# Left-over queries scored on 64 rows in the AV banks, and some loads issued later, in an attention + maxout FFN kernel

## The chip, the cores and the metric

One core of a Trainium2 chip runs the whole program. The metric is the device time of one execution in microseconds (us), and smaller is better. A kernel is run several times, and its median and range are given. The profile is of one of these runs. Where two kernels are compared by a ratio, it is the mean time of one kernel's fast runs over the mean time of the other's fast runs of the same rounds on the same chip, so it isn't quite the ratio of the medians that stand beside it. All runs in this document were in the fast state but one of the six of e5 (327.61 us), which its ratio leaves out and its median does not. All kernels gave a correct result.

Engines in the profile: PE is TensorE, PEld its weight loads, ACT is ScalarE, DVE is VectorE, POOL is GpSimd (it issues most of the loads), SP is SyncE (it issues transposes by DMA and stores).

## The reference, cut to what matters

Eight batches, eight heads, 576 positions, head size 64; then a three-way maxout FFN on the 4608 tokens.

```python
scores = scale * np.matmul(q, k.transpose(0, 1, 3, 2)) + bias      # bias depends on |i - j| only
attn = np.exp(scores - max); attn = attn / sum(attn)
x = (attn @ v).transpose(0, 2, 1, 3).reshape(4608, 512)
h = np.maximum(np.maximum(x @ w1, x @ w2), x @ w3)                 # d_ff = 768
out = h @ w_out
```

576 is four tiles of 128 and 64 left over. So each pair of heads has full tiles of keys and queries, left-over keys and left-over queries. The bias is applied as a multiplication after the exponential ("band products" on VectorE). The FFN of one batch runs on PE between the attention products of the next.

## The kernel before: the parts that matter

A head pair has two visits (query halves c = 0 and 1). Each makes scores in two `sc` tiles, exponentials on ScalarE, band products on VectorE, and then a "filling": FFN work put on PE while the other engines deal with the scores. Three PSUM pools of two buffers each matter: one for scores (`sc`, also used by `sct`, left-over keys, and `scq`, left-over queries), one for attention outputs (`a`, the "AV banks") and one for the FFN (`ff`).

```python
ps_s = ctx.enter_context(tc.tile_pool(name="ps_s", bufs=2, space=bass.MemoryType.PSUM))   # sc, sct, scq
ps_a = ctx.enter_context(tc.tile_pool(name="ps_a", bufs=2, space=bass.MemoryType.PSUM))   # a
ps_f = ctx.enter_context(tc.tile_pool(name="ps_f", bufs=2, space=bass.MemoryType.PSUM))   # ps0, ps1, ps2, pso
...
# one portion of filling: third product of the last block, first and second of this one
portions.append([g[fb - 1], f[fb], m[fb]])      # g: ps2 -> hT (DVE max); f: ps0 -> m0 (ACT copy); m: ps1 -> m (DVE max)
...
def left_queries(hp, qT, kT, el):
    sc = ps_s.tile([P, KT, 2 * 64], F32, tag="sc", name="scq")
    for t in range(KT):                       # both heads at once, half of the 128 rows times zeros
        mm(sc[:, t, :], lhsT=kT[:, P * t : P * t + P], rhs=qT[:, QM : QM + P])
    eq = el[:, S + 64 :].rearrange("p (t h q) -> p t h q", t=KT, h=2)
    exp(eq, sc[:].rearrange("p t (h q) -> p t h q", h=2))
...
for b, hp in ...:                             # main loop, cut
    visit(qT, kT, e4, 0)
    quotients = next_late()                   # AV products of the pair before, first half
    times_band(hp, e4, 0, 0, QS, inorder)
    quotients()
    fill(rate, lambda: left_keys(hp, qT, kT, el, 0, S + 64))
    visit(qT, kT, e4, 1)
    quotients = next_late()                   # AV products, second half
    times_band(hp, e4, 1, 0, QM, inorder)     # the band product that stands ahead of hT on VectorE
    quotients()
    ...
    def queries():
        left_queries(hp, qT, kT, el)
        times_band(hp, e4, 3, 0, QM, inorder)
    fill(rate, lambda: times_band(hp, e4, 2, 0, QM, inorder), queries)
```

Everything on PE and VectorE is pinned to this order (`inorder`).

The softmax here doesn't subtract the row's maximum and nothing guards it: scores larger than these inputs give would overflow.

Of the kernel before, what the change touches and what calls it, by code (L numbers as in the profile page):

```python
# [39 lines left out]
def kernel(  # L40
# [77 lines left out]
    def constants(i):  # L118
        inorder(nc.vector.memset(ktail[i][:], 0.0))
        if i == 0:  # L120
            inorder(nc.vector.memset(qtail[i][:], 0.0))
        inorder(nc.vector.memset(vt[i][:], 0.0))
        inorder(nc.vector.memset(vx[i][:, :, :, D:AW], 1.0))
        for par in range(2):
            inorder(nc.vector.memset(vt[i][64 * par : 64 * par + 64, :, par, D:AW], 1.0))
# [7 lines left out]
    def in_turn(b, load):  # L133
        return inorder(load) if b > 2 else load

    def load_main(src, b, h0, h1, dst, t0=0, t1=KT):
        x = main_part(src, b)
        if h1 - h0 < KT:
            for h in range(h0, h1):
                nc.gpsimd.dma_start(out=dst[:, :, h, :], in_=x[:, :, h, :])  # L140
        else:
            for t in range(t0, t1):
                in_turn(b, nc.gpsimd.dma_start(out=dst[:, t, h0:h1, :], in_=x[:, t, h0:h1, :]))  # L143
# [5 lines left out]
    def q_diag(b, par, h0, h1):  # L149
        return diag(qtail[b % 2], par, h0, h1)  # L150
# [7 lines left out]
    def load_tail(src, b, h0, h1, dst):  # L158
        for par in range(2):
            in_turn(b, nc.gpsimd.dma_start(out=dst(b, par, h0, h1), in_=tail_part(src, b, h0, h1, par)))  # L160

    def load_qk(b, behind=None):
# [5 lines left out]
        for src, dst in ((q, q_diag), (k, k_diag)):  # L168
            for par in range(2):
                load = nc.gpsimd.dma_start(out=dst(b, par, 0, H), in_=tail_part(src, b, 0, H, par))  # L170
                loads.append(in_turn(b, load))
        if behind:
            for load in loads:
                tc.add_manual_dep(
                    load.ins, behind.ins.name,
                    mybir.DependencyInfo(mybir.DependencyClass.Sync, mybir.DependencyReason.DATA),
                    reason="these loads go behind the result's transposes",
                )

    def load_v(b, h0, h1):  # L180
        load_main(v, b, h0, h1, vx[b % 2][:, :, :, 0:D])
        load_tail(v, b, h0, h1, v_diag)
# [61 lines left out]
    inorder(nc.vector.memset(qtail[1][:], 0.0))  # L244
# [17 lines left out]
    load_tail(q, 0, 0, H, q_diag)  # L262
# [40 lines left out]
    bandt = const.tile([P, HP, 2 * P], BF16, name="bandt")  # L303

    def make_bandt():
        for par in range(2):
            r = slice(64 * par, 64 * par + 64)
            c = BAND // 2 - 64 * par
            for c0, c1 in ((192, 256), (0, 192)):
                dve_copy(bandt[r, :, c0:c1], hank[r, par::2, c : c + c1 - c0][:, :, ::-1])  # L310
# [4 lines left out]
    def ffn(t0, nt, last):  # L315
# [76 lines left out]
        else:  # L392
# [3 lines left out]
            portions.append(o[:1])  # L396
# [4 lines left out]
    pending, rest, stores = [], [], []  # L401
# [36 lines left out]
    def transposes(b):  # L438
# [4 lines left out]
        def one(j, t):  # L443
            src = batch[b][j][:, t].rearrange("p h d -> p (h d)") if t < KT else (
                (qtail, ktail)[j][b % 2][:].rearrange("p h c -> p (h c)")
            )
            inorder(nc.sync.dma_start_transpose(out=made[j][:, :, P * t : P * t + P], in_=src))
# [6 lines left out]
    def qk_tiles():  # L454
        return [qkt.tile([P, HP, (KT + 1) * P], BF16, tag=n, name=n) for n in ("qT", "kT")]
# [25 lines left out]
    def more_transposes(hp):  # L481
# [6 lines left out]
        dve_copy(qk[0][0][:, hp, QS:], tp[:, 0 : QS + P])  # L488

    def second_transposes(made, hp):  # L490
# [3 lines left out]
        for j, tl in enumerate((qtail, ktail)):  # L494
# [11 lines left out]
            copy(made[j][:, hp, KT * P :], tp[:, j, KT * P : (KT + 1) * P])  # L506
            for j, copy in enumerate((dve_copy, act_copy))
# [16 lines left out]
    def visit(qT, kT, e4, c, mid=None):  # L524


        for tt in range(0, KT, 2):
# [23 lines left out]
    def times_bandt(hp, el):  # L551
        inorder(nc.vector.tensor_tensor(
            out=el[:, S - 192 : S + 64], in0=el[:, S - 192 : S + 64], in1=bandt[:, hp, :], op=ALU.mult
        ))

    def left_queries(hp, qT, kT, el):

        sc = ps_s.tile([P, KT, 2 * 64], F32, tag="sc", name="scq")
        for t in range(KT):
# [314 lines left out]
```

## Time and profile before

| kernel before | |
|---|---|
| time, median of 4 runs (3 of them known when the prediction was made) | 325.96 us (323.77 to 326.36) |
| span of the profiled run | 324.3 us |
| PE busy | 310.4 us, 96% of the span |
| one batch in the steady part (start of batch five to start of batch six) | 33.88 us |
| longest wait of PE | 3.43 us, at 16.3 to 19.7 us, on the values' tail `vt` |
| half-speed stretches of PE's clock | two of 3.41 us, from 19.59 and 29.83 us (granted clock 0.50 in both) |

Busy shares tell that PE is the engine whose stream is the time, and the start of the same instruction in two successive batches gives the length of a batch without any adding up. Most lines of the page and the timelines are in the prediction below. One row that it doesn't show, of the costliest groups (after the bars: busy us, mean ns of one, idle us before them and what ended it):

```profile
L94 PE MATMUL ps<-xT,w_bf 128*128 128x512 bf16 (+1 forms) x720 | 156.4, 359 | 0.0
```

Half of PE's busy time is these FFN products, and PE never waited in front of one. In a timeline the columns are start, duration, engine, source line, operation, written tile <- read tiles, shapes, count, and in brackets the idle time before with what ended it.

### The profile page before, as it was taken

How to read it: one execution, taken by the hardware profiler on the slowest of the kernel's cores; microseconds unless marked ns; L12 is line 12 of the kernel's file. 1: busy time of each engine (PE TensorE's matmuls, PEld its weight loads, DVE VectorE, ACT ScalarE, POOL GpSimd, SP SyncE). 2: the span in 40 equal slices, each digit the busy share in tenths (PEclk: the TensorE clock that was granted, in tenths of full speed). 3: DMA queues.
4: the chain of work that ended last, by engine and by line, in shares of the span. 5: the costliest groups of instructions: out<-in, count | busy, mean ns of one | idle time of the engine just before them, and what ended most of it. 6: DMA issues, size and time to landing. Idle time of an engine off the chain costs nothing.

```text
span 324.3 us, 8019 instructions
## 1 busy us (share of the span) xinstructions
PE 310.4 (96%) x3232; PEld 177.1 (55%) x3232; DVE 216.0 (67%) x537; ACT 201.8 (62%) x274; POOL 112.6 (35%) x151
## 2 busy tenths in 40 slices
PE   7757999999999999999999999999999999999995
PEld 2345776787555555555555555555555554444442
DVE  6476787777666766676667766777767675454452
ACT  3947798798677667776777677667776651121221
POOL 8941977109857852194109700500000000000000
PEclk9978999999999999999999999999999999999999
DMA  9999999949999999999989998996032003301103
GB/s 163 188 207 198 154 162 153 164 109 127 192 160 155 159 181 168 118 129 164 200 81 127 175 209 76 104 205 119 1 73 98 35 3 73 132 0 65 67 0 129
DMA packets 165541, 40.72 MB, mean 126 GB/s; under 512 B 155384, under 2 KB 161024, under 8 KB 165504
## 3 DMA queue, kind: packets, MB, share of 16 engines
q0 software_dynamic: 103904, 16.66, 74.8%
q1 hardware_dynamic: 59840, 23.08, 38.7%
q10 hardware_dynamic: 1760, 0.47, 0.6%
q8 instruction: 25, 0.41, 0.5%
q14 instruction: 12, 0.10, 0.1%
HBM read 35.39 MB, written 9.45 MB: 138 GB/s over the span
## 4 chain that ended last, share of the span: by engine, by line
PE 86%; ACT 4%; POOL 3%; DMA 3%; DVE 2%; issue 1%; POOLq 0%; ACTq 0%
PE ps L94 42%; PE a L94 15%; PE pso L94 14%; PE sc L94 9%; ACT e L522 3%; PE sct L94 3%; PE scq L94 2%; DMA vt<-in_v_dram 2%; POOL q_sb L143 1%; POOL vx L143 1%; PE tp L97 1%; DMA out_dram<-osb 1%; DVE e L516 1%; ACT el L522 1%; POOL qtail L160 0%
## 5 line engine op out<-in xcount | busy, mean ns | idle before, releaser
L94 PE MATMUL ps<-xT,w_bf 128*128 128x512 bf16 (+1 forms) x720 | 156.4, 359 | 0.0
L522 ACT ACTIVATE e<-sc 128x1024 bf16<-128x1024 f32 x128 | 124.3, 1026 | 24.7 <-PE sc L94 24.1
L94 PEld LDWEIGHTS <-w_bf 128*128 128x128 bf16 x720 | 66.1, 98 | 57.1 <-issue 1.5
L516 DVE TENSOR_TENSOR e<-e,hank 128x512 bf16<-128x512 bf16 (+2 forms) x136 | 59.7, 467 | 26.9 <-ACT e L522 24.9
L337 ACT ACTIVATE m<-ps 128x512 bf16<-128x512 f32 x54 | 32.3, 598 | 66.0 <-PE ps L94 63.7
L343 DVE TENSOR_TENSOR m<-ps,m 128x512 bf16<-128x512 f32 x54 | 37.3, 690 | 45.7 <-ACT el L522 25.8
L94 PEld LDWEIGHTS <-kT 64*128 64x128 bf16 (+1 forms) x704 | 35.7, 96 | 38.6 <-issue 22.8
L94 PE MATMUL pso<-wo_bf,hT 128*128 128x512 bf16 (+2 forms) x222 | 51.0, 373 | 0.0
L94 PE MATMUL a<-vx,e 128*128 128x65 bf16 x1024 | 46.4, 195 | 0.0
L94 PE MATMUL a<-vt,el 128*128 128x130 bf16 (+1 forms) x192 | 40.3, 216 | 3.4 <-DMA vt<-in_v_dram 3.4
L143 POOL DMA_DIRECT2D vx<-in_v_dram x32 | 28.3, 892 | 43.4 <-PE a L94 38.5
L94 PE MATMUL sc<-qT,kT 64*128 64x256 bf16 x512 | 40.6, 272 | 2.4 <-DVE kT L110 1.0
L94 PEld LDWEIGHTS <-e 128*128 128x128 bf16 x1024 | 42.0, 99 | 1.0 <-issue 0.2
L348 DVE TENSOR_TENSOR hT<-ps,m 128x512 bf16<-128x512 f32 x54 | 37.0, 685 | 4.9 <-PE ps L94 3.1
L609 DVE TENSOR_TENSOR x_sb<-a,rd 128x256 bf16<-128x256 f32 (+1 forms) x64 | 31.4, 491 | 2.2
L94 PEld LDWEIGHTS <-el 128*128 128x128 bf16 x448 | 24.5, 98 | 14.8 <-issue 10.3
L94 PEld LDWEIGHTS <-hT 128*128 128x128 bf16 x222 | 20.2, 98 | 20.6 <-DVE hT L348 0.4
L110 DVE COPY osb<-pso 128x512 f32<-128x512 f32 (+1 forms) x33 | 22.7, 687 | 13.2 <-PE pso L94 9.4
L167 POOL DMA_DIRECT2D q_sb<-in_q_dram x24 | 22.2, 924 | 17.2 <-DVE x_sb L609 15.3
L522 ACT ACTIVATE el<-sct 128x640 bf16<-128x640 f32 (+2 forms) x36 | 23.2, 647 | 5.5 <-PE sct L94 4.9
L167 POOL DMA_DIRECT2D k_sb<-in_k_dram x24 | 22.0, 916 | 5.3 <-DMA vx<-in_v_dram 3.8
L522 ACT ACTIVATE el<-scq 128x512 bf16<-128x512 f32 x32 | 19.0, 595 | 6.6 <-PE scq L94 6.6
(69 smaller groups left out, 169.8 us busy)
## 6 DMA issues: line engine op xcount, KB each, us to landing
out_dram<-osb SPq DMA_DIRECT2D x35, 256.0 KB, 3.3
vx<-in_v_dram POOLq DMA_DIRECT2D x32, 128.0 KB, 6.2
q_sb<-in_q_dram POOLq DMA_DIRECT2D x26, 128.0 KB, 8.0
k_sb<-in_k_dram POOLq DMA_DIRECT2D x24, 128.0 KB, 8.9
w_bf<-in_moe_w_dram POOLq DMA_DIRECT2D x3, 768.0 KB, 13.4
xT<-in_k_dram SPq DMA_DIRECT2D x6, 128.0 KB, 4.6
hank<-w_dr SPq DMA_DIRECT2D x2, 384.0 KB, 6.2
wo_bf<-in_moe_w_out_dram POOLq DMA_DIRECT2D x1, 768.0 KB, 7.9
```

Source lines behind the costliest of these rows:

```text
L94: inorder(nc.tensor.matmul(*args, **kw))
L97: inorder(nc.tensor.transpose(*args))
L110: return inorder(nc.vector.tensor_copy(out_, in_))
L143: in_turn(b, nc.gpsimd.dma_start(out=dst[:, t, h0:h1, :], in_=x[:, t, h0:h1, :]))
L167: loads.append(in_turn(b, nc.gpsimd.dma_start(out=dst[:, t], in_=main_part(src, b)[:, t])))
L337: nc.scalar.activation(out=st[fb]["m0"][:], in_=ps0, func=ACTF.Copy)
L343: inorder(nc.vector.tensor_tensor(out=m[:], in0=ps1, in1=st[fb]["m0"][:], op=ALU.max))
L348: inorder(nc.vector.tensor_tensor(out=hT[:, fb * CH : fb * CH + CH], in0=ps2, in1=st[fb]["m"][:], op=ALU.max))
L516: put(nc.vector.tensor_tensor(out=e4[:, t, :, lo:hi], in0=e4[:, t, :, lo:hi], in1=hank[:, 2 * hp : 2 * hp + 2, c0:c1][:, :, ::-1], op=ALU. ...
L522: nc.scalar.activation(out=out_, in_=in_, func=ACTF.Exp, scale=inv_sqrt_d)
L609: divided[b, hp, half] = inorder(nc.vector.tensor_tensor(out=x_sb[b][:, 2 * half : 2 * half + n, P * hp : P * hp + P].rearrange("p t (h d) ...
```

## The change

Its intent: the four left-over-query products of 128 rows were half zeros. They become eight products of 64 rows and 64 columns, which can stand directly in front of the second visit's scores (the same 64-row form, so no change of form for them alone; between 128 and 64 rows one took 0.10 us each way in the trace of the kernel before). For that they are put in the two AV banks, and these have to be free, so the second AV group moves forward, to the filling after the first visit. Besides, the left-over queries of a batch are loaded by one DMA instead of two; the output weights' load goes behind the q and k loads of batch three; batch three's values are loaded behind its transposes; the first output products are deferred. The diff's core:

```diff
+    def load_q_tail(b):                       # one DMA, plain layout, 64 partitions
+        dst = qtail[b % 2][0 : S - KT * P].rearrange("p g (h d) -> p (g h) d", h=2)
+        return in_turn(b, nc.gpsimd.dma_start(out=dst, in_=q[b, :, KT * P : S, :].rearrange("h p d -> p h d")))
...
+    def put_left_queries(el, banks):
+        eq = el[:, S:].rearrange("p (t h q) -> p t h q", t=KT, h=2)
+        for par, bank in enumerate(banks):
+            exp(eq[:, :, par, :], bank.rearrange("p (t q) -> p t q", t=KT))
+    def turn_left_queries(qT, kT, banks):
+        for t in range(KT):
+            for par, bank in enumerate(banks):
+                r = slice(64 * par, 64 * par + 64)
+                mm(bank[:, 64 * t : 64 * t + 64], lhsT=kT[r, P * t : P * t + P], rhs=qT[r, QM:S])
+    def visit(qT, kT, e4, c, mid=None, el=None):
+        if el is not None:
+            banks = [ps_a.tile([P, KT * 64], F32, tag="a", name="scq") for _ in range(2)]
+            turn_left_queries(qT, kT, banks)
+            put_left_queries(el, banks)
         for tt in range(0, KT, 2):
... main loop:
+        together = b > 1 and (b, hp) != (2, 0)
-        fill(rate, lambda: left_keys(hp, qT, kT, el, 0, S + 64))
+        fill(
+            rate, *([lambda: next_late()()] if together else []),
+            lambda: left_keys(hp, qT, kT, el, 0, S),
+        )
-        visit(qT, kT, e4, 1)
+        visit(qT, kT, e4, 1, el=el if together else None)
-        quotients = next_late()
+        quotients = None if together else next_late()
         times_band(hp, e4, 1, 0, QM, inorder)
-            load_v(b + 1, 0, H)
+            load_v(b + 1, 0, H, turned_qk[2, 1, KT - 1] if b == 1 else None)
         def queries():
-            left_queries(hp, qT, kT, el)
+            if not together:
+                left_queries(hp, qT, kT, el)
... (tile sizes, tails of 64 instead of 128 columns, deferred outputs, load_last_weights: cut)
```

In what follows, a "joint visit" is a second visit that starts with its left-over queries: 23 of the 32, all of batches three to eight but the first pair. In 17 of them the filling behind is three FFN products; in five it is twelve matmuls of output products, and in the first of all it is six.

More of the change, by code (lines that the diff above doesn't have):

```diff
@@ L120, in constants @@
         if i == 0:
-            inorder(nc.vector.memset(qtail[i][:], 0.0))
+            inorder(nc.vector.memset(qtail[i][64:, :, :], 0.0))
         inorder(nc.vector.memset(vt[i][:], 0.0))
@@ L133, in in_turn @@
     def in_turn(b, load):
-        return inorder(load) if b > 2 else load
+        return inorder(load)
     def load_main(src, b, h0, h1, dst, t0=0, t1=KT):
         x = main_part(src, b)
-        if h1 - h0 < KT:
-            for h in range(h0, h1):
-                nc.gpsimd.dma_start(out=dst[:, :, h, :], in_=x[:, :, h, :])
-        else:
-            for t in range(t0, t1):
-                in_turn(b, nc.gpsimd.dma_start(out=dst[:, t, h0:h1, :], in_=x[:, t, h0:h1, :]))
+        return [
+            in_turn(b, nc.gpsimd.dma_start(out=dst[:, t, h0:h1, :], in_=x[:, t, h0:h1, :])) for t in range(t0, t1)
+        ]
     def diag(dst, par, h0, h1):
@@ L147, in diag @@
         return dst[r, h0 // 2 : h1 // 2, r]
-    def q_diag(b, par, h0, h1):
-        return diag(qtail[b % 2], par, h0, h1)
+    def load_q_tail(b):
+        dst = qtail[b % 2][0 : S - KT * P].rearrange("p g (h d) -> p (g h) d", h=2)
+        return in_turn(b, nc.gpsimd.dma_start(out=dst, in_=q[b, :, KT * P : S, :].rearrange("h p d -> p h d")))
     def k_diag(b, par, h0, h1):
@@ L158, in load_tail @@
     def load_tail(src, b, h0, h1, dst):
-        for par in range(2):
+        return [
             in_turn(b, nc.gpsimd.dma_start(out=dst(b, par, h0, h1), in_=tail_part(src, b, h0, h1, par)))
+            for par in range(2)
+        ]
     def load_qk(b, behind=None):
@@ L167, in load_qk, with go_behind, load_v @@
                 loads.append(in_turn(b, nc.gpsimd.dma_start(out=dst[:, t], in_=main_part(src, b)[:, t])))
-        for src, dst in ((q, q_diag), (k, k_diag)):
-            for par in range(2):
-                load = nc.gpsimd.dma_start(out=dst(b, par, 0, H), in_=tail_part(src, b, 0, H, par))
-                loads.append(in_turn(b, load))
-        if behind:
-            for load in loads:
-                tc.add_manual_dep(
-                    load.ins, behind.ins.name,
-                    mybir.DependencyInfo(mybir.DependencyClass.Sync, mybir.DependencyReason.DATA),
-                    reason="these loads go behind the result's transposes",
-                )
-    def load_v(b, h0, h1):
-        load_main(v, b, h0, h1, vx[b % 2][:, :, :, 0:D])
-        load_tail(v, b, h0, h1, v_diag)
+        loads.append(load_q_tail(b))
+        for par in range(2):
+            load = nc.gpsimd.dma_start(out=k_diag(b, par, 0, H), in_=tail_part(k, b, 0, H, par))
+            loads.append(in_turn(b, load))
+        go_behind(loads, behind)
+    def go_behind(loads, behind):
+        for load in loads if behind else ():
+            tc.add_manual_dep(
+                load.ins, behind.ins.name,
+                mybir.DependencyInfo(mybir.DependencyClass.Sync, mybir.DependencyReason.DATA),
+                reason="these loads go behind the transposes in line",
+            )
+    def load_v(b, h0, h1, behind=None):
+        loads = load_main(v, b, h0, h1, vx[b % 2][:, :, :, 0:D])
+        go_behind(loads + load_tail(v, b, h0, h1, v_diag), behind)
     xT = const.tile([P, DCH, NTOK], BF16, name="xT")
@@ L243 @@
     constants(0)
-    inorder(nc.vector.memset(qtail[1][:], 0.0))
+    inorder(nc.vector.memset(qtail[1][64:, :, :], 0.0))
     dve_copy(pick[:], ids[:])
@@ L261 @@
     load_main(q, 0, 0, H, batch[0][0], 2, KT)
-    load_tail(q, 0, 0, H, q_diag)
+    load_q_tail(0)
     load_v(0, 0, H)
@@ L299, in load_hank @@
         ))
-    bandt = const.tile([P, HP, 2 * P], BF16, name="bandt")
+    bandt = const.tile([P, HP, 192], BF16, name="bandt")
     def make_bandt():
@@ L308, in make_bandt @@
             c = BAND // 2 - 64 * par
-            for c0, c1 in ((192, 256), (0, 192)):
-                dve_copy(bandt[r, :, c0:c1], hank[r, par::2, c : c + c1 - c0][:, :, ::-1])
+            dve_copy(bandt[r, :, :], hank[r, par::2, c : c + 192][:, :, ::-1])
     def ffn(t0, nt, last):
@@ L395, in ffn @@
                 portions += [[f[fb]], [m[fb], g[fb]]]
-            portions.append(o[:1])
+            if t0:
+                portions += [[x] for x in deferred]
+                portions.append(o[:1])
+            else:
+                deferred.extend(o)
+                o = []
         if len(o) > 2:
@@ L399, in ffn @@
         return portions, o[-1:]
-    pending, rest, stores = [], [], []
+    pending, rest, stores, deferred = [], [], [], []
     def store_outputs():
@@ L443, in one @@
         def one(j, t):
+            n = P if t < KT or j else S - KT * P
             src = batch[b][j][:, t].rearrange("p h d -> p (h d)") if t < KT else (
-                (qtail, ktail)[j][b % 2][:].rearrange("p h c -> p (h c)")
+                (qtail, ktail)[j][b % 2][0:n].rearrange("p h c -> p (h c)")
             )
-            inorder(nc.sync.dma_start_transpose(out=made[j][:, :, P * t : P * t + P], in_=src))
+            turned_qk[b, j, t] = inorder(nc.sync.dma_start_transpose(out=made[j][:, :, P * t : P * t + n], in_=src))
         for t in range(KT + 1):
@@ L454, in qk_tiles @@
     def qk_tiles():
-        return [qkt.tile([P, HP, (KT + 1) * P], BF16, tag=n, name=n) for n in ("qT", "kT")]
+        return [qkt.tile([P, HP, n], BF16, tag=x, name=x) for x, n in (("qT", S), ("kT", (KT + 1) * P))]
     def first_transposes(hp):
@@ L487, in more_transposes @@
         tr(tp[:, QS : QS + P], qtail[0][:, hp, :], ident[:])
-        dve_copy(qk[0][0][:, hp, QS:], tp[:, 0 : QS + P])
+        dve_copy(qk[0][0][:, hp, QS:], tp[:, 0 : S - QS])
     def second_transposes(made, hp):
@@ L505, in second_transposes @@
         tail = [
-            copy(made[j][:, hp, KT * P :], tp[:, j, KT * P : (KT + 1) * P])
-            for j, copy in enumerate((dve_copy, act_copy))
+            copy(made[j][:, hp, KT * P :], tp[:, j, KT * P : n])
+            for j, (copy, n) in enumerate(((dve_copy, S), (act_copy, (KT + 1) * P)))
         ]
@@ L522, in exp @@
         nc.scalar.activation(out=out_, in_=in_, func=ACTF.Exp, scale=inv_sqrt_d)
-    def visit(qT, kT, e4, c, mid=None):
+    def put_left_queries(el, banks):
[12 more added lines that the diff above has]
+            put_left_queries(el, banks)
         for tt in range(0, KT, 2):
@@ L552, in times_bandt @@
         inorder(nc.vector.tensor_tensor(
-            out=el[:, S - 192 : S + 64], in0=el[:, S - 192 : S + 64], in1=bandt[:, hp, :], op=ALU.mult
+            out=el[:, S - 192 : S], in0=el[:, S - 192 : S], in1=bandt[:, hp, :], op=ALU.mult
         ))
     def left_queries(hp, qT, kT, el):
-        sc = ps_s.tile([P, KT, 2 * 64], F32, tag="sc", name="scq")
-        for t in range(KT):
-            mm(sc[:, t, :], lhsT=kT[:, P * t : P * t + P], rhs=qT[:, QM : QM + P])
-        eq = el[:, S + 64 :].rearrange("p (t h q) -> p t h q", t=KT, h=2)
-        exp(eq, sc[:].rearrange("p t (h q) -> p t h q", h=2))
+        sc = ps_s.tile([P, 2, CH], F32, tag="sc", name="scq")
+        turn_left_queries(qT, kT, [sc[:, par, 0 : KT * 64] for par in range(2)])
+        eq = el[:, S:].rearrange("p (t h q) -> p h t q", t=KT, h=2)
+        exp(eq, sc[:, :, 0 : KT * 64].rearrange("p h (t q) -> p h t q", t=KT))
     def times_band_left(hp, el):
-        last_tile = el[:, S + P * KT - 64 :].rearrange("p (h q) -> p h q", h=2)
+        last_tile = el[:, S + P * KT - P :].rearrange("p (h q) -> p h q", h=2)
         inorder(nc.vector.tensor_tensor(
@@ L568, in times_band_left @@
         ))
-    divided = {}
+    divided, turned_qk = {}, {}
     def attend(b, hp, e4, el, half):
@@ L593, in attend @@
         if half:
+            mm(
+                x[:, 4:6, :], lhsT=el[:, S - P : S], rhs=vl[:, hp, :, 0:AW],
+                start=True, stop=False, skip_group_check=True,
+            )
             for par in range(2):
-                mm(
-                    x[:, 4 + par, :], lhsT=el[:, S - P + 64 * par :][:, 0:P], rhs=vl[:, hp, par, 0:AW],
-                    start=True, stop=False, skip_group_check=True,
-                )
                 for kt in range(KT):
                     mm(
-                        x[:, 4 + par, :], lhsT=el[:, S + P * kt + 64 * par :][:, 0:P],
+                        x[:, 4 + par, :], lhsT=el[:, S - 64 + P * kt + 64 * par :][:, 0:P],
                         rhs=v[:, kt, 2 * hp + par, 0:AW],
@@ L643, in e_tiles @@
             ep.tile([P, KT, 2, QM], BF16, tag="e4", name="e4"),
-            ep.tile([P, S + 64 + KT * P], BF16, tag="el", name="el"),
+            ep.tile([P, S + KT * P], BF16, tag="el", name="el"),
         )
@@ L659 @@
         wb = const.tile([P, DCH, d_ff], BF16, name=f"w{i}_bf")
-        nc.gpsimd.dma_start(out=wb[:], in_=wk.rearrange("(c p) f -> p c f", p=P))
+        in_turn(0, nc.gpsimd.dma_start(out=wb[:], in_=wk.rearrange("(c p) f -> p c f", p=P)))
         w_bf.append(wb)
@@ L669, in load_second @@
             if h0 == 0:
-                load_tail(q, 1, 0, H, q_diag)
+                load_q_tail(1)
                 load_tail(k, 1, 0, H, k_diag)
@@ L673, in load_second, with load_last_weights @@
         load_v(1, 0, H)
-        nc.gpsimd.dma_start(out=wo_bf[:], in_=moe_w_out.rearrange("(c p) m -> p c m", p=P))
+    def load_last_weights():
+        in_turn(0, nc.gpsimd.dma_start(out=wo_bf[:], in_=moe_w_out.rearrange("(c p) m -> p c m", p=P)))
     def bands(hp):
@@ L734, in keys @@
         def keys():
-            left_keys(hp, qT, kT, el, QS, S + 64)
+            left_keys(hp, qT, kT, el, QS, S)
         def queries():
@@ L759 @@
                 load_qk(2)
+                load_last_weights()
                 x_transposes(0, 1)
@@ L794 @@
             spread_packed(hp + 1, nc.vector)
-        fill(rate, lambda: left_keys(hp, qT, kT, el, 0, S + 64))
+        fill(
+            rate, *([lambda: next_late()()] if together else []),
+            lambda: left_keys(hp, qT, kT, el, 0, S),
+        )
         times_bandt(hp, el)
-        visit(qT, kT, e4, 1)
+        visit(qT, kT, e4, 1, el=el if together else None)
         store_outputs()
@@ L805 @@
             turned.pop(0)()
-        quotients = next_late()
+        quotients = None if together else next_late()
         times_band(hp, e4, 1, 0, QM, inorder)
-        quotients()
+        if quotients:
+            quotients()
         if b == 1 and hp + 1 < HP:
```

## The prediction

> **What bounds the kernel now.** I read the page first (busy shares, the forty slices, the chain that ended last), then the timeline of each engine over one head pair of the steady part, then the first 30 us.
>
> ```profile
> PE 310.4 (96%) x3232; PEld 177.1 (55%) x3232; DVE 216.0 (67%) x537; ACT 201.8 (62%) x274; POOL 112.6 (35%) x151
> ...
> PE   7757999999999999999999999999999999999995
> ...
> PEclk9978999999999999999999999999999999999999
> ...
> PE 86%; ACT 4%; POOL 3%; DMA 3%; DVE 2%; issue 1%; POOLq 0%; ACTq 0%
> ```
>
> TensorE (PE) is busy in every slice after the first seven, and the chain runs through it for 86% of the span. So a microsecond counts only if it shortens PE's stream or makes PE wait. In the steady part a batch takes 33.88 us (the same place of the pattern at 109.41, 143.30 and 177.18 us). The question is whether PE has slack against the two engines that empty its PSUM banks. One visit of the second query half:
>
> ```profile
> 117.71 0.61 PE L94 MATMUL sc<-qT,kT 64*128 64x256 bf16 x8
> 118.25 0.23 PE L94 MATMUL a<-vt,el 128*128 128x130 bf16 x1
> ...
> 119.16 1.89 PE L94 MATMUL ps<-xT,w_bf 128*128 128x512 bf16 x8
> 120.88 0.39 PE L94 MATMUL scq<-qT,kT 128*128 128x128 bf16 x4
> 121.11 1.03 PE L94 MATMUL ps<-xT,w_bf 128*128 128x512 bf16 x4
> 122.07 0.61 PE L94 MATMUL sc<-qT,kT 64*128 64x256 bf16 x8
> ```
>
> ```profile
> 117.17 0.70 ACT L522 ACTIVATE el<-sct 128x640 bf16<-128x640 f32 x1
> 118.14 1.94 ACT L522 ACTIVATE e<-sc 128x1024 bf16<-128x1024 f32 x2 [0.27 <-PE sc L94]
> ```
>
> ```profile
> 119.20 0.56 DVE L516 TENSOR_TENSOR e<-e,hank 128x768 bf16<-128x768 bf16 x1 [0.42 <-ACT e L522]
> 119.67 0.19 DVE L608 RECIPROCAL rd<-a 128x6 f32<-128x6 f32 x1
> 119.89 0.56 DVE L609 TENSOR_TENSOR x_sb<-a,rd 128x384 bf16<-128x384 f32 x1
> 120.37 0.68 DVE L348 TENSOR_TENSOR hT<-ps,m 128x512 bf16<-128x512 f32 x1
> ```
>
> Read the three together. PE does 8 scores (0.54 us), the AV products (0.91), two FFN products (four matmuls each, 1.72 together), the left-over scores scq (0.23) and a third FFN product (0.86 plus a gap of 0.10). Call the three FFN products g, f, m. They share two banks, so m, at 121.11, goes where g was, and g is emptied by the hT row, which ends at 120.37 + 0.68 = 121.05. There is no visible wait, and only 0.06 us of slack. The hT row is late because it stands in VectorE's order behind the band product at 119.20, which waits for the first score exponential (118.14 plus 1.03).
>
> [...]m of four 512-column matmuls takes 0.96 us start to start before 64-row scores (121.11 to 122.07) against 0.86 elsewhere, and eight score matmuls (four pairs at once, 4 x 0.107) take 0.54. So a switch costs 0.10 us each way. [...]the four scq take 0.225 us (56 ns each), eight AV products 0.24 us (30 ns). [...]
>
> **The change, part by part.**
>
> *Left-over scores.* Four matmuls of 128 rows and 128 columns, half of them zeros, become eight of 64 rows and 64 columns, in pairs on the two row halves. [...]In 23 of the 32 visits (all of batches three to eight but the first) they stand directly before the second visit's scores, already in 64-row mode: no new switch. There they save 0.025 us each. In the other 9 they stand alone among 128-row matmuls: two new switches, 0.20 + 0.20 - 0.225 = +0.18 us each; four of these are in batch one, where PE idles anyway.
>
> *Smaller left-over keys.* sct falls from 640 to 576 columns: 27 ns of PE per visit, some 55 ns of ScalarE (640 columns take 702 ns, 512 of scq 595, so 0.83 ns a column). The band product on el loses 64 of 256 columns on VectorE, off the path. AV of the left-over queries goes from ten matmuls of 65 columns to one of 130 and eight of 65: 10 x 30 = 300 against 60 + 240 = 300 ns. Nothing.
>
> So PE's own work falls by 0.05 us in 23 visits (-1.2 us) and rises by 0.15 in nine (+1.4, of which I count 1.0).
>
> *The AV banks.* The scq pair needs both AV banks empty, so the second AV group is moved forward into the filling after the first visit. After the second visit PE then runs g, f, m with nothing between, as the order of the changed program confirms: 17 times it has twelve 512-column products in a row right after the scores (five times twelve output products). ScalarE now has two scq exponentials ahead of the two score exponentials. VectorE's order is still band product, then hT; the reciprocal and quotient before hT are gone. The changed program's waits still tie m to that hT.
>
> The walk, with t = 0 at the first scq:
> - ScalarE starts the first scq exponential at about 0.40 (before, a score exponential started 0.43 after the first score). A 256-column exponential takes 0.41 us, and a following one starts 0.1 before its end (1.94 for two of 1.026), so two occupy 0.62: score exponential at 1.02, done at 2.04.
> - VectorE: band product at 2.07, hT 0.47 later (119.20 to 119.67), done at 2.54 + 0.68 = 3.22. PE can start m at 3.28.
> - PE: scq 0.20, scores with exit 0.55, g 0.86, f 0.86: ready for m at 2.47.
>
> PE waits 0.81 us, 17 times: +13.8 us. In the old order AV (0.91) and scq (0.23) lay between, and the exponential came 0.6 earlier; this is what the change takes away. For output products the bank two back is copied out ahead of the band product, so I expect no wait in those five. The m0 copy on ScalarE (about 2.85 to 3.45) and the max after m do not hold the next visit: its AV banks and score slots are long free. The ordinary first visit gets longer filling (both AV groups) and has slack. So the period of such a head pair goes from 8.47 to about 9.2 us.
>
> *Loads.* The left-over queries are loaded by one DMA, not two. PE's longest early wait is on the values' tail:
>
> ```profile
> 19.72 0.27 PE L94 MATMUL a<-vt,el 128*128 128x130 bf16 x1 [3.43 <-DMA vt<-in_v_dram]
> ...
> 7.41 1.27 POOL L160 DMA_DIRECT2D qtail<-in_q_dram  x2
> 8.64 3.57 POOL L143 DMA_DIRECT2D vx<-in_v_dram  x4
> 12.16 1.30 POOL L160 DMA_DIRECT2D vt<-in_v_dram  x2
> ```
>
> One issue fewer (0.63) starts vt that much sooner, but it lands 6.8 us after issue with the queues full and the same bytes ahead of it; I count -0.5 us. Output weights and batch three's values come later, but the first output product also moves later (the first outputs are deferred to the second FFN part), and after 57 us no PE wait on a DMA of theirs exists to remove. I count zero.
>
> Sum: 326.1 + 13.8 - 1.2 + 1.0 - 0.5 = 339.2. I take off about a microsecond, as some of the 17 waits will be shorter than the walk: **338.0 us**.
>
> **Rivals.** (a) PE-only reading: no wait arises, the kernel gains 1 to 3 us from less PE work and an earlier start: 323 to 325. For it: the change looks like a step of tuning, and each moved piece is small. Against it: the 0.06 us slack before[...]. (b) Start-up: if vt lands a microsecond sooner, the clock dip (slices 3 and 4, granted 0.79 and 0.84) may shrink and give 2 to 3 us; this would add to either outcome: 336, or 321. For it: the dip follows the 3.4 us idle. Against: bytes, not issues, seem to limit. (c) The late loads come too late and PE waits for the output weights or for batch three's values: +2 to +5 us on top. Against: values are needed near 85 us, and their load is some 6 us long, issued from about 65 us. (d) The waits are longer, since ScalarE's strided stores or VectorE's backlog also hold f: 1.1 us each, 343.
>
> **Range and chances.** The 17 waits at 0.6 to 0.95 us give 10 to 16 us; with start-up of plus or minus 2 the range is 331.0 to 342.0. Over 2% slower is above 332.6: 0.82. Within 2%: 0.15, mostly rival (a) or half-size waits. Faster by 2% would need 319.6, which no part pays for: 0.03.
>
> **What would show it.** Right: in batches three to eight, an idle time on PE of about 0.8 us before one `ps` group per visit, released by VectorE's hT row, absent before; a batch near 36.2 us, not 33.9; [...]PE's busy share down by three or four points. Wrong: PE full to the end with a batch under 34 us (rival a); hT before the band product in the trace; a PE wait on a DMA between 60 and 90 us (c); the vt wait under 2.5 us and no clock dip (b).

## The result, and the profile after

The changed kernel takes 335.22 us (median of 4 runs, 333.84 to 337.8), the kernel before 325.96. The ratio of the fast runs is 1.031, with a 95% interval of 1.023 to 1.0385: slower. The predicted time was 338.0 and the range 331 to 342.

From the page of the changed kernel: busy time by engine, the chain that ended last by engine, and the row of the FFN products with the idle time before them in the last column.

```profile
PE 308.1 (93%) x3288; PEld 171.6 (52%) x3328; DVE 213.6 (64%) x535; ACT 199.5 (60%) x297; POOL 108.0 (33%) x143
...
PE 63%; ACT 14%; DVE 7%; DMA 7%; issue 4%; POOL 3%; POOLq 0%; ACTq 0%
...
L94 PE MATMUL ps<-xT,w_bf 128*128 128x512 bf16 (+1 forms) x694 | 153.7, 357 | 12.4 <-DVE hT L350 9.9
```

PE's share falls from 96% to 93%, and the chain now leaves PE for ScalarE and VectorE (86% on PE before). Before, the `ps` row had no idle time. (Forty matmul records are missing in this trace, 3288 of 3328, which is why a few groups count three or seven instead of four or eight; small "issue" gaps beside them aren't real waits.) The view of PE's waits has one line for the cause (columns: total us, times, longest):

```profile
PE ps L94 <- DVE hT L350: 9.9, 17, 0.6
```

Seventeen waits, one per joint visit with FFN filling. Here is one of them, on PE, ScalarE and VectorE of the changed kernel:

```profile
127.50 0.29 PE L94 MATMUL scq<-qT,kT 64*128 64x64 bf16 x8
127.63 0.60 PE L94 MATMUL sc<-qT,kT 64*128 64x256 bf16 x8
128.16 1.90 PE L94 MATMUL ps<-xT,w_bf 128*128 128x512 bf16 x8
130.64 1.02 PE L94 MATMUL ps<-xT,w_bf 128*128 128x512 bf16 x4 [0.58 <-DVE hT L350]
131.60 0.61 PE L94 MATMUL sc<-qT,kT 64*128 64x256 bf16 x8
```

```profile
127.82 0.66 ACT L530 ACTIVATE el<-scq 128x256 bf16<-128x256 f32 x2 [0.19 <-PE scq L94]
128.37 1.95 ACT L530 ACTIVATE e<-sc 128x1024 bf16<-128x1024 f32 x2
```

```profile
129.43 0.56 DVE L524 TENSOR_TENSOR e<-e,hank 128x768 bf16<-128x768 bf16 x1 [0.90 <-ACT e L530]
129.91 0.68 DVE L350 TENSOR_TENSOR hT<-ps,m 128x512 bf16<-128x512 f32 x1
```

Follow the arrows backwards. The third FFN product `m` starts at 130.64. It goes into the bank of the first, `g`, which hT empties; hT ends at 129.91 + 0.68 = 130.59. hT stands behind the band product of 129.43, which had VectorE idle for 0.90 us until the first score exponential was done. That exponential starts at 128.37, behind two scq exponentials. On PE nothing lies between the scores and g, f, m any more.

How long is the wait? The bracket says 0.58. But the first eight products start at 128.16, and eight at 0.2155 us each put the next start at 129.89; it comes at 130.64, so 0.75 us are lost. The difference is in the lengths that the trace shows, which reach past the next start: groups of four such products are shown 1.02 to 1.03 us long, while the next group starts 0.86 us after their start. So lengths of PE waits are taken from start to start here: 17 x 0.75 = 12.8 us.

The start-up is where the changed kernel wins. Its loads on POOL, and the first product that needs the values' tail:

```profile
7.31 0.78 POOL L148 DMA_DIRECT2D qtail<-in_q_dram  x1
...
11.54 1.30 POOL L158 DMA_DIRECT2D vt<-in_v_dram  x2
```

```profile
18.55 0.22 PE L94 MATMUL a<-vt,el 128*128 128x130 bf16 x1
```

The tail is issued 0.62 us sooner (12.16 before) and has landed by 18.42 instead of 19.59. In this run PE waits nowhere for it, and no half-speed stretch of the clock follows (granted 1.00 over the span). (How much of the start's gain this explains is weighed below, under the prediction.) Where the time went in the profiled runs, by the start of the first score product of each batch, changed minus before:

| start of | before, us | after, us | difference |
|---|---|---|---|
| batch two | 38.40 | 35.00 | -3.40 |
| batch three | 66.89 | 63.44 | -3.45 |
| batch four | 96.66 | 96.04 | -0.62 |
| batch five | 130.54 | 131.60 | +1.06 |
| length of a steady batch | 33.88 | 35.57 | +1.69 |
| end of the span | 324.3 | 332.1 | +7.8 |

So the joint visits begin in batch three, and the start has given 3.4 us before that. From batch four on they cost 1.7 us a batch. Batch three loses 2.8 us: 1.5 by two of the 17 waits, and about 0.85 by the deferral, which moves twelve output matmuls of 512 columns in and sixteen FFN matmuls of 256 columns out (12 x 0.2155 - 16 x 0.109; batch two has as much less, but was not shorter: 28.44 us against 28.49). Whether the deferral costs anything as a whole, no run tells.

### The profile page after: what moved, and what is told of

Its sections match the earlier page's. It is cut to its first block, busy times and chain, and to the rows that moved or that the text cites. A ratio compares the mean times of both kernels' runs of the same rounds, so it can differ in the third digit from the quotient of the medians.

```text
span 332.1 us, 8194 instructions
## 1 busy us (share of the span) xinstructions
PE 308.1 (93%) x3288; PEld 171.6 (52%) x3328; DVE 213.6 (64%) x535; ACT 199.5 (60%) x297; POOL 108.0 (33%) x143
## 4 chain that ended last, share of the span: by engine, by line
PE 63%; ACT 14%; DVE 7%; DMA 7%; issue 4%; POOL 3%; POOLq 0%; ACTq 0%
PE ps L94 30%; PE pso L94 13%; PE a L94 13%; ACT e L530 8%; PE sc L94 6%; DMA xT<-in_q_dram 5%; DVE hT L350 4%; DVE m L345 3%; ACT el L530 3%; ACT m L339 3%; DMA vx<-in_v_dram 1%; PE sct L94 1%; POOL q_sb L139 1%; PE scq L94 1%; PE tp L97 1%
## 5 line engine op out<-in xcount | busy, mean ns | idle before, releaser
L94 PE MATMUL ps<-xT,w_bf 128*128 128x512 bf16 (+1 forms) x694 | 153.7, 357 | 12.4 <-DVE hT L350 9.9
L94 PEld LDWEIGHTS <-w_bf 128*128 128x128 bf16 x720 | 64.1, 97 | 73.5 <-issue 19.8
L94 PEld LDWEIGHTS <-kT 64*128 64x128 bf16 (+1 forms) x832 | 30.0, 95 | 36.1 <-issue 25.8
L94 PE MATMUL pso<-wo_bf,hT 128*128 128x512 bf16 (+2 forms) x208 | 47.7, 373 | 0.8 <-issue 0.2
L94 PE MATMUL a<-vx,e 128*128 128x65 bf16 x1024 | 44.5, 193 | 0.0
L94 PE MATMUL sc<-qT,kT 64*128 64x256 bf16 x512 | 41.8, 278 | 2.2 <-ACT e L530 0.9
L94 PEld LDWEIGHTS <-e 128*128 128x128 bf16 x1024 | 40.5, 97 | 3.0
L94 PE MATMUL a<-vt,el 128*128 128x130 bf16 x160 | 35.6, 222 | 0.0
L530 ACT ACTIVATE el<-scq 128x256 bf16<-128x256 f32 (+1 forms) x55 | 20.5, 416 | 9.9 <-PE scq L94 9.7
L530 ACT ACTIVATE el<-sct 128x576 bf16<-128x576 f32 (+2 forms) x36 | 21.4, 598 | 6.9 <-PE sct L94 6.8
```

What stands on the lines that cost most here:

```text
L94: inorder(nc.tensor.matmul(*args, **kw))
L530: nc.scalar.activation(out=out_, in_=in_, func=ACTF.Exp, scale=inv_sqrt_d)
```

## The experiments

Theory A (the prediction's): the loss is the wait of `m` for hT. It has two roots, namely the AV and scq work taken away from in front of g, f, m, and the score exponential delayed by the two scq exponentials. Rival B: something else in the joint visits costs (ScalarE's strided stores, more instructions on it, or the late loads), and the hT wait is only where it shows. Ten kernels were run, all from the changed kernel with one edit (or two, where said). Ratios are to the kernel before in the same rounds. Times by batch and waits are of one profiled run each. The last column is the time lost in front of `m`, from start to start.

| run | edit | median, us | before, us | ratio (95%) | steady batch, us | hT wait, us |
|---|---|---|---|---|---|---|
| changed | - | 335.22 | 325.96 | 1.031 (1.023 to 1.0385) | 35.57 | 0.75 |
| e1 | band product behind hT | 325.77 | 326.05 | 0.996 (0.989 to 1.002) | 33.57 | 0.08 |
| e2 | score exponentials first | 329.25 | 326.05 | 1.011 (1.004 to 1.018) | 34.60 | 0.43 |
| e3 | second AV group back | 333.59 | 326.05 | 1.022 (1.018 to 1.026) | 35.05 to 35.88 | 0.46 |
| e4 | one more scq exponential | 339.73 | 326.05 | 1.041 (1.037 to 1.045) | 36.40 | 1.02 |
| e5 | e1 + batch five's q, k later | 325.27 (fast runs alone 323.93) | 326.05 | 0.995 (0.991 to 1.000) | 33.57 | 0.08 |
| e6 | e1 + loads as before | 330.30 | 326.05 | 1.012 (1.007 to 1.018) | 33.57 | 0.08 |
| e7 | no joint visits | 329.16 | 326.05 | 1.009 (1.006 to 1.012) | 34.19 | none |
| e8 | left-over queries by two DMAs | 336.54 | 326.05 | 1.034 (1.028 to 1.039) | 35.57 | 0.75 |
| e9 | e1 + batch four's values held | 322.94 | 327.29 | 0.988 (0.983 to 0.993) | 33.57 | 0.08 |
| e10 | e9, batch three's values free | 329.49 | 325.57 | 1.011 (1.007 to 1.015) | 33.57 | 0.08 |

### e1: only the order on VectorE

```diff
-        times_band(hp, e4, 1, 0, QM, inorder)
+        if not together:
+            times_band(hp, e4, 1, 0, QM, inorder)
 ...
-        fill(rate, lambda: times_band(hp, e4, 2, 0, QM, inorder), queries)
+        def middle():                                  # called behind g's hT
+            if together:
+                times_band(hp, e4, 1, 0, QM, inorder)
+            times_band(hp, e4, 2, 0, QM, inorder)
+        fill(rate, middle, queries)
```

> Edit: in the 23 joint visits the second half's first band product is put behind the emptying of the first FFN product (hT) in VectorE's order; nothing else changes. Theory (hT stands behind a band product that waits for ScalarE): hT can start as soon as g is done, so the 17 waits of PE on hT, now 0.75 us each beyond the matmul's own time, fall to under 0.15; 11 to 12.5 us are won, median 322 to 325, a steady batch 33.2 to 33.5 us. Rival 1 (two banks are simply too few for three products in a row, whatever VectorE's order): hT still ends 0.5 us or more after m could start, under 4 us won, 331 or more. Rival 2 (the late loads or the deferred outputs cost the time): no change, 335.

The wait of 0.75 us shrinks to 0.08. VectorE of this run shows why: hT waits for its own product on PE and the band products come after it.

```profile
130.98 0.69 DVE L350 TENSOR_TENSOR hT<-ps,m 128x512 bf16<-128x512 f32 x1 [0.70 <-PE ps L94]
131.59 1.40 DVE L524 TENSOR_TENSOR e<-e,hank 128x768 bf16<-128x768 bf16 x3
```

A steady batch takes 33.57 us, less than before the change (33.88). Not one byte, matmul or exponential was taken away, so rival B's extra ScalarE work is not what cost the time. But the total, 325.8, misses the expectation on the high side. In the profiled run (326.93, the longest of the four) a new wait is the reason:

```profile
98.01 0.39 PE L94 MATMUL sc<-qT,kT 64*128 64x256 bf16 x2 [2.49 <-DMA kT<-k_sb]
```

The last two scores of batch four's first visit wait for the transposed keys. PE's clock is at half speed from 97.69 us for 3.41 us, and this batch takes 37.66 us instead of 33.57. In the changed kernel the same transpose lands at 95.47 us, and these scores start at 96.38: a second weakness, 0.9 us from showing (in the kernel before it lands at 96.75, for scores at 97.00). Two things moved in e1. The scores were due 0.86 us sooner, at 95.52, since the hT waits were gone; and the transpose landed 2.5 us later, at 97.96. Why it landed later, this run alone doesn't tell.

### e2, e3 and e4: the two roots, and a dose

e2 lets ScalarE make the score exponentials before the scq exponentials (the order pinned):

```diff
             turn_left_queries(qT, kT, banks)
-            put_left_queries(el, banks)
         for tt in range(0, KT, 2):
             ...
+        if el is not None:
+            put_left_queries(el, banks)
```

> Edit: ScalarE makes the two score exponentials of the joint visit ahead of the two left-over ones; VectorE's order as in the changed kernel. Theory: the band product, and hT behind it, come about 0.55 us earlier, so each of the 17 waits falls from 0.75 to about 0.2 us: 9 us won, median 325 to 328. Rival 1 (banks): waits stay over 0.6, 333 or more. Rival 2 (loads, deferred outputs): no change, 335.

e3 puts the second AV group back behind the second visit's scores, and leaves the scq pair where the change has it:

```diff
-        fill(rate, *([lambda: next_late()()] if together else []), lambda: left_keys(hp, qT, kT, el, 0, S))
+        fill(rate, lambda: left_keys(hp, qT, kT, el, 0, S))
...
-        quotients = None if together else next_late()
+        quotients = next_late()
```

> Edit: the second AV group goes back between the second visit's scores and the filling, as in the kernel before; the left-over scores stay in front of the scores in the AV banks. Theory: m becomes ready 0.91 us later, but the reciprocal and quotient (0.70 us) again stand ahead of hT, and the two left-over exponentials still delay the band product, so the wait only falls from 0.75 to about 0.5 us: 4 us won, median 329 to 333. Rival (the removed AV work was all that hid hT, ScalarE's order is nothing): waits vanish, 322 to 325.

e4 makes the first scq exponential twice; its result is the same:

```diff
+            put_left_queries(el, banks[:1])
             put_left_queries(el, banks)
```

> Edit: the changed kernel with the first left-over exponential made twice (same values written again), a dose of ScalarE work ahead of the score exponentials in the 23 joint visits. Theory: every one of the 17 waits grows by one exponential's spacing, 0.28 us (0.66 for two of 0.38), to about 1.03: 4.8 us longer, median 339 to 341; the five output fillings stay without a wait. Rival (ScalarE's time is hidden, the wait is VectorE's or the banks' own): under 1 us longer, 335 to 336.

The line of the hT waits in the view of PE's waits, for e2, e3 and e4:

```profile
PE ps L94 <- DVE hT L350: 4.4, 17, 0.3
```

```profile
PE ps L94 <- DVE hT L350: 5.0, 17, 0.3
```

```profile
PE ps L94 <- DVE hT L350: 14.6, 17, 0.9
```

e4 hit: one more ScalarE instruction in front lengthens each wait from 0.75 to 1.02 us and the batch from 35.57 to 36.40 (3 x 0.27 = 0.81). So ScalarE's order in front of the band product is on the path at its full length. e2 missed its time by about a microsecond. The wait was 0.43, not 0.2: I had counted the whole 0.55 us between the starts of the first scq exponential and the first score exponential, but the latter cannot start before its own scores, and it came only about 0.33 earlier. In e3 the wait was 0.46 as expected (0.5) and the time just above the expected range. PE has 0.9 us more to do in front of m, but the reciprocal and the quotient also return in front of hT on VectorE; and there were waits of 1.0 and 1.1 us for batch four's keys and another of 0.7 us. Each root taken back alone leaves more than half of the wait; the order on VectorE alone (e1) removes nearly all of it.

### e5: are batch five's loads what delays batch four's keys?

e1, and batch five's q and k loads held behind that very transpose:

```diff
-            load_qk(b + 2)
+            load_qk(b + 2, turned_qk[b + 1, 1, KT - 1] if b == 2 else None)
```

> Edit: as e1_band_after, and batch five's q and k are loaded behind the key transposes of batch four's last full tile, so that they do not share the DMA engines with them. In e1 the steady batches took 33.57 us (33.88 before), but batch four's first scores waited 2.5 us for the transposed keys, and the clock then ran at half speed for 3.4 us. Theory (this wait is contention with the loads of batch five, and it ate what e1 won): the wait falls under 0.5 us, batch four goes from 37.7 to about 33.6 us, median 320.5 to 323, faster than both kernels by 1 to 1.5% of before. Rival (the transposes are late for another reason, their own issue or batch three's late values): the wait stays over 1.5 us, 325 to 326.

My theory fell, by the profiled run. These loads now started at 98.16 us, and yet the transpose landed at 97.61 and the wait stayed 2.3 us. (The times alone could not decide: the five fast runs lie between 322.62 and 326.63 us, and only the slowest of them was traced.) The rival was left: batch four's own values, issued from 78.36 us and landing from 89.5 to 97.9, beside its own transposes.

### e6: e1 with the loads as before

```diff
-            load_v(b + 1, 0, H, turned_qk[2, 1, KT - 1] if b == 1 else None)
+            load_v(b + 1, 0, H)
...   # output weights loaded in start-up again, first output products not deferred
```

> Edit: as e1_band_after, with the output weights, batch three's values and the first outputs put back to where the kernel before has them. Theory (the late loads are not what makes batch four's keys late: the DMA engines have room at 62 to 70 us, where the late values go): the wait for the transposed keys stays at 1 us or more, median 324 to 326.5. Rival (the late values displaced batch four's loads): the wait vanishes and the median is 321 to 323.

A miss, in a direction that I had not expected: the early loads make it worse. PE waits for transposed keys three times (6.4 us together, the longest 3.2), and there are half-speed stretches from 68.49 and 102.63 us. The change's later loads, together with the deferred outputs, are then a gain once the hT waits are gone: 0.996 for e1 against 1.012 for this. Whether they gain anything in the changed kernel as it stands, where the waits delay the need, no run tells.

### e7: the whole change but the joint visits

```diff
-        together = b > 1 and (b, hp) != (2, 0)
+        together = False
```

> Edit: the changed kernel with no joint visit: the left-over scores (64 rows) always on their own in the score banks, the second AV group after the second visit as before; loads as changed. Theory: none of the 17 waits on hT, for the old order of PE, ScalarE and VectorE is back; left-over scores on their own pay two mode switches, so a steady batch takes 33.88 + 4 x (0.13 + 0.20 - 0.225 - 0.027) = 34.2 us; with the better start (about 3 us) the median is 324 to 328, more if batch four's keys are late as in e1. Rival (the 64-row scores themselves or the loads cost the time): 333 or more.

No hT waits and a batch of 34.19, as expected. Its excess of 0.31 over before is the form switch of four lone scq groups: 4 x (0.13 + 0.20 - 0.225 - 0.027) = 0.31. The total misses. In the profiled run batch three's values, held behind its transposes, come 1.8 us late (PE waits from 70.76 to 72.57 us), with a half-speed stretch of 3.41 us after it (from 73.17 us), and batch three takes 34.73 us instead of e1's 31.26. The clock isn't needed for the miss, though: two of the other runs were granted 1.0 and took 328.61 and 329.18 us.

### e8: the left-over queries' load alone

```diff
-        return in_turn(b, nc.gpsimd.dma_start(out=dst, in_=q[b, :, KT * P : S, :]...))
+        return [in_turn(b, nc.gpsimd.dma_start(out=dst[:, h : h + KT], in_=q[b, h : h + KT, KT * P : S, :]...)) for h in (0, KT)]
```

> Edit: the changed kernel with the left-over queries loaded by two DMAs of four heads instead of one of eight. Theory (the start gains because one GpSimd issue of about 0.6 us less stands ahead of the values): the values' tail is issued 0.5 us later and lands 0.5 to 1.2 us later, 19 us or after, PE's wait for it grows by as much, and the median is 0.5 to 3 us longer than the changed kernel's, 335.5 to 338. Rival[...]: no later landing, 334 to 336.

```profile
7.34 1.29 POOL L148 DMA_DIRECT2D qtail<-in_q_dram  x2
...
12.18 1.27 POOL L158 DMA_DIRECT2D vt<-in_v_dram  x2
```

```profile
20.94 0.22 PE L94 MATMUL a<-vt,el 128*128 128x130 bf16 x1 [3.37 <-DMA vt<-in_v_dram]
```

A hit by the traces. With the second DMA back the tail is issued 0.64 us later, lands at 20.81 instead of 18.42, and the wait of 3.4 us is there again. Batch two starts at 36.83 instead of 35.00; in the nine other kernels with the one DMA it starts between 34.94 and 35.83. So the one DMA is worth 1 to 2 us in the profiled starts. In the total it is not clear of the noise: the two ratios, 1.034 and 1.031, have intervals that overlap.

### e9: batch four's values held as well

e1, and batch four's values held behind the last transpose of its keys' full tiles, in the way that the change holds batch three's:

```diff
-        if hp == (2, 1, 0)[min(b, 3) - 1] and b + 1 < B:
-            load_v(b + 1, 0, H, turned_qk[2, 1, KT - 1] if b == 1 else None)
+        if hp == (2, 2, 0)[min(b, 3) - 1] and b + 1 < B:
+            load_v(b + 1, 0, H, turned_qk[b + 1, 1, KT - 1] if b < 3 else None)
```

> Edit: as e1_band_after, and batch four's values (not batch five's q and k) are loaded behind the key transposes of batch four's last full tile. In e5 batch five's loads were held to 98 us, yet that key transpose still landed at 97.6 us, together with the values (issued from 78 to 86 us, landed 89.5 to 97.9). Theory (the transposes share the DMA engines with batch four's own values): the transpose lands before 95 us, PE's wait for it falls under 0.5 us, batch four takes about 33.6 us, median 320.5 to 323, faster than both kernels. Rival (the transposes are slow whatever runs beside them, or the held values now come late): a wait of 1.5 us or more for keys or values stays, 325 to 327.

```profile
PE 308.9 (96%) x3328; PEld 171.6 (53%) x3328; DVE 213.5 (66%) x535; ACT 199.2 (62%) x297; POOL 108.3 (33%) x143
```

PE is busy for 96% of the span again, and its view of waits has neither keys nor hT in it. A hit: the transpose lands at 92.18, the wait for keys is gone, and batch four takes 33.57 us like the others. On POOL batch five's q and k stand behind the values, so they start late here too (at 97.46 us). The run to compare is therefore e5, where they also start late and only the values run beside the transpose. The time from issue to landing of this one transpose, in e5 and in e9:

```profile
DMA to landing us min/median/max: 9.7/9.7/9.7
```

```profile
DMA to landing us min/median/max: 2.4/2.4/2.4
```

To two digits that is 9.66 and 2.45 us. This kernel is faster than both: 322.94 us against 327.29 of the kernel before on the same chip, 1.2% by the ratio (0.7 to 1.7).

### e10: and batch three's values freed again

```diff
-            load_v(b + 1, 0, H, turned_qk[b + 1, 1, KT - 1] if b < 3 else None)
+            load_v(b + 1, 0, H, turned_qk[b + 1, 1, KT - 1] if b == 2 else None)
```

> This is the run before (band product behind the hT row, batch four's values held behind its keys' transposes) with batch three's values no longer held behind batch three's transposes, as in the kernel before. There a second wait of PE of about 1.6 us on the values' tail fell in batch three's time. If holding batch three's values is a pure cost of the change, that wait goes, nothing new comes, and the time falls from a ratio of 0.988 against the kernel before to 0.981 to 0.985 (321 to 322.5 us where the kernel before takes 327.3). Rival: freed, these values crowd batch three's own transposes on the same DMA engines, as batch four's did before they were held; then a wait of PE on kT or qT of 1 us or more appears at batch three's start, with or without a half-speed stretch after it, and the ratio is 0.99 to 1.00.

In e9 PE still waits 1.58 us for batch three's values (71.25 to 72.83 us, with no half-speed stretch after it), and I expected to gain that. The rival was right, and the loss was larger than even it had said:

```profile
67.54 0.66 PE L94 MATMUL sct<-qT,kT 128*128 128x512 bf16 x2 [2.75 <-DMA kT<-ktail]
```

The values' wait goes, but they now move beside batch three's transposes. The last one (the keys' tail) lands at 67.49 instead of 65.42, PE waits 2.75 us, and from 66.58, within this wait, the clock is at half speed for 6.83 us, twice as long as elsewhere. Batch three takes 36.5 us instead of 32.89. Holding batch three's values, as the change does, is therefore a gain in this kernel. In the profiled runs this accounts for the whole difference in span (326.0 against 323.2 us: +3.6 here, -0.8 in the start). The medians differ by more, and what the other runs of e10 lost besides was not looked at.

## Why the prediction was right, and where its sizes were off

**No slack, and the strict order on VectorE: right.** The step from "0.06 us of slack" to a wait of m for hT held in every part: its releaser, its place, its number (17), its absence in the five output fillings. e1 shows the cause by removing the wait with a reordering alone. That ScalarE's order counts as well, e4 shows: one more exponential in front took each wait from 0.75 to 1.02 us.

**The walk: right within 0.15 us.** Predicted from the first scq on: score exponential at 1.02, band product at 2.07, hT done at 3.22, m at 3.28, PE ready at 2.47. Measured (the first scq is at 127.50): 0.87, 1.93, 3.09, 3.14 and 2.39. The wait is 0.75 instead of 0.81, and the sum 12.8 instead of 13.8. The microsecond that I took off at the end came to just that, though for another reason: all 17 waits are alike. Rival (a), no wait, and rival (d), waits of 1.1 us, are both out. The batch came to 35.57 us instead of "near 36.2": about 0.2 of it from the waits (3 x 0.06), about 0.3 from PE's own work, which comes next; some 0.15 stays open.

**PE's own work: mis-sized.** I counted 200 ns for the scq group (0.20 in the walk), an estimate that no trace showed; much of the -1.2 and +1.0 us in the sum rested on it. The group takes 0.13 us (127.50 to 127.63), 16 ns each on the mean. My own reading of the scores, four pairs at once (eight matmuls in 0.54 us, a switch of 0.10 included), should have warned me. So a joint visit saves 0.095 + 0.027 = 0.12 us instead of 0.05, and the nine others lose 0.08 instead of 0.15: -2.8 + 0.7 = -2.1 us instead of -0.2.

**The start: mis-sized.** I counted -0.5 us for one issue less and wrote that bytes, not issues, seem to limit. In the profiled runs it was -3.4. The medians differ by 9.3 us; with +12.8 and -2.1 that leaves about -1.4 for the start and all else. e8 shows that the single DMA is worth 1 to 2 us of the 3.4.

The rest doesn't come from the tail's earlier landing: its first product starts only 1.17 us sooner in the profiled run (18.55 against 19.72), and 2.2 us are gained behind it. In nine other kernels with the one DMA, PE still waits for the tail, by 0.8 to 2.8 us, and eight of them have a half-speed stretch in the start; yet batch two starts 2.6 to 3.5 us sooner than before. In e9 the tail's product even starts later than before, at 20.18 us instead of 19.72. From this product to batch two it is 18.68 us in the run before, and 15.65 to 16.64 in all the others, e8 included. In that stretch the run before has this wait of PE, at 28.0 to 29.5 us, and its second half-speed stretch, from 29.83:

```profile
PE xp L97 <- ACT xT L107: 1.5, 1, 1.5
```

For ScalarE's `xT` the others wait at most 0.8 us, and they have no half-speed stretch between 26 and 66 us. Which of the start's edits does it was not tested, and there is but one profile of the kernel before, so this part is seen, not shown by an experiment. Rival (b) was thus partly true, on top of the main outcome, as it had said itself.

**Late loads: right for the changed kernel, and incomplete.** No wait of PE on a DMA appears between 60 and 90 us in it, and none for output weights. But "I count zero" hid that batch four's keys land only 0.57 us before their batch, and 0.9 us before their scores. With the hT waits gone the scores were due 0.86 us sooner and the keys landed 2.5 us later (e1). And the traffic that delays transposes is the values loaded beside them (9.66 us to landing in e5 against 2.45 in e9, and a wait of 2.75 us in e10), which neither I nor the diff's wording had put first.

With these terms the sum reads 326 + 12.8 - 2.1 - 1.4 = 335.3; the last term is what was left over, so that the sum agrees is no proof of it. In the two profiled runs, with the measured 3.4 us of the start, it is 12.8 - 2.1 - 3.4 = 7.3 against the measured 7.8; the 0.5 stays open.

## What to carry to other kernels

When a change moves work out of a place, ask what that work was covering: here 1.1 us of PE work had covered an evacuation of a PSUM bank that stood behind another engine's wait in a strict order. If such a wait appears, look first at the order on the evacuating engine, since putting the evacuation ahead of the item that waits took nothing away and left 0.08 of 0.75 us. And a removed wait brings every later need forward (here by 0.86 us), so look at what lands just in time; in this kernel what crowded it were the values' loads issued beside transposes by DMA (the same transpose took 9.66 us to land beside them in e5 and 2.45 us without them in e9).
